# Scores of the third to sixth block: one head's 64 rows at a time, into two banks, instead of a zero-padded operand

## Chip, core and metric

One core of one Trainium2 chip. Times are microseconds on the device for one execution of the program; several executions are timed and their median is given. One further execution is profiled, and all rows below are of that one.

## What is computed

Three stages in a row. The first is a gated linear recurrence over a sequence (a state-space layer) with 4 batches, 8 heads, 768 positions, head width 32 and state width 16; the reference does it in chunks of 32 positions:

```
L = exp(cum[:, None] - cum[None, :]) * causal
M = einsum('bhin,bhjn->bhij', Cc, Bc) * L          # scores times decay
y[:, :, sl] = M @ xc + (Cc @ state) * exp(cum)     # within the chunk + from the state
state = decay_full * state + sum_j B_j x_j * decay_from_j
```

The heads are joined to 3072 tokens of 256 features. Then comes an RMS norm and a gated MLP (256 to 1536 and back, silu), then a second MLP (256 to 2048 and back, softplus). All inputs are fp32.

## The kernel before

**Tiling.** The recurrence runs in chunks of 128 positions: 6 blocks of the sequence by 4 batches are 24 *units*, unit u being block u // 4 of batch u % 4. The two MLPs run over 6 blocks of 512 tokens, one per four units. Their matrices are split into a high and a low part of a short-mantissa fp32 type (F32R), and a product is made of matmuls of high by high, low by high and high by low parts, each with 128 rows, 128 columns of weights and 512 streamed columns. They are the bulk of TensorE's work: PSUM tiles `p` (first layers) and `t` (second layers).

**A unit** (`unit`, L536). It loads the decays of 8 heads (`ab`), scans them into triangles of running products (L607), computes the scores of the 8 heads (L631 to L647), multiplies scores and decays (L656, *decay*, two halves `s` of four heads), and then runs a group *products* (L677 to L695): `inter` (state times C, one matmul per half of the heads, on 64 rows each), `state` and `intra` (32 columns of weights each). From the third block on, two units share one group of products. The scores' two PSUM banks (`gps`) and the products' two banks (`ybanks`) come from one pool `a` of two banks.

**Scores before.** Units 0 to 7 are *native* (`nat`): per head a matmul of 16 rows (the state width) in fp32, which the chip does as two passes. Units 8 to 23, the third to sixth block, use F32R pieces that `split` (L521) has written to DRAM (`parts`): per unit 128 rows by 4 pairs of heads by 128 positions for the one operand (`st`), and as much for the other (`cz`). The upper 64 rows are one head of each pair, the lower 64 the other; within a half, a row is a state index and one of four pieces of the split product. So that one matmul of 128 rows can do both heads of a pair without mixing them, `cz` holds each half of the rows beside zeros: it is 128 rows by 4 pairs by 2 by 128, where `cz[64z:64z+64, q, z]` holds data (L584, two loads) and the rest is zeroed once by GpSimd at the start (L1146). The four matmuls (`pairs`, L643) stream 256 columns each, both heads of pair q side by side. Two pairs go to each bank, so a bank holds the heads in another order than `ab` does; the decay reads `ab` by a rearranged view (L654) and counts both halves of `ab` as read and written (L657). Two `cz` tiles take turns; at the end of the program they hold MLP operands (L950).

**Order.** Every operation is registered with its engine, an estimated time, a rank, and what it reads and writes. A planner (`Plan`) simulates the engines, picks an order for each queue from ranks and due times in eight passes, and keeps the best. At the start (`LEAD`, `plan.now`) an order written by hand holds. TensorE (PE), VectorE (DVE), ScalarE (ACT) and GpSimd (POOL) each run their own list in order. Nearly all DMAs are issued by one queue, SP. The planner's estimate for a set of `pairs` is 4 x 125 ns (L647).

Of the kernel before, what the change touches and what calls it, by code (L numbers as in the profile page):

```python
# [8 lines left out]
F32R = mybir.dt.float32r  # L9
# [5 lines left out]
ALU = mybir.AluOpType  # L15
AX = mybir.AxisListType

P = 128
NB, NH, SEQ, HD, NS = 4, 8, 768, 32, 16
# [308 lines left out]
def tile_ssd_then_swiglu_then_softplus_mlp(  # L328
# [10 lines left out]
    nc = tc.nc  # L339
    act, dve, pool, pe = nc.scalar, nc.vector, nc.gpsimd, nc.tensor  # L340
    plan = Plan(LAT)
# [4 lines left out]
    def buf(tag, shape, dt=F32, bufs=1):  # L346
        if bufs not in pools:
            pools[bufs] = ctx.enter_context(tc.tile_pool(name=f"sb{bufs}", bufs=bufs))
        return plan.buf(pools[bufs], bufs, tag, shape, dt)
# [5 lines left out]
    def pbuf(tag, shape):  # L355
        p, n = {"p": (ps_p, 4), "a": (ps_a, 2), "t": (ps_t, 2)}[tag]
        return plan.buf(p, n, tag, shape, F32)

    def mm(o, l, r, start, stop):
        pe.matmul(out=o, lhsT=l, rhs=r, start=start, stop=stop, skip_group_check=True)  # L360
# [12 lines left out]
    def PE(ns, rank, fn, r=(), w=(), cols=0):  # L373
        plan.op({"pe": (ns, fn)}, rank, r, w, cols)
# [7 lines left out]
    def pool_ns(n):  # L382
        return 150 + n * 2.1

    def DVE(n, rank, fn, r=(), w=(), fast=False, port=True, ns=None):
        plan.op({"dve": (ns or dve_ns(n, fast), fn) + (("port",) if port else ())}, rank, r, w)
# [4 lines left out]
    def POOL(n, rank, fn, r=(), w=()):  # L391
        plan.op({"pool": (pool_ns(n), fn, "port")}, rank, r, w)
# [14 lines left out]
    def LOAD(kb, rank, fn, w, r=()):  # L407
        plan.op({"sp": (kb * DMA_NS, fn)}, rank, r, w)
# [13 lines left out]
    cz = [const.tile([P, 4, 2, P], F32, name=f"cz{i}") for i in range(2)]  # L422
# [9 lines left out]
    parts = [dram.tile([2, P, 4, 4 * P], F32, name=f"parts{t}") for t in range(UPB)]  # L432
# [17 lines left out]
    for layer, t in seq:  # L450
        b = blocks[t]
# [84 lines left out]
    def unit(u):  # L536
        nat = u < NATIVE
        blk, b = divmod(u, NB)
# [6 lines left out]
        def at(name):  # L545
            plan.now = None if blk_of[u] else LEAD[name][o]
        rank = [base]

        def nxt(k=1):
            rank[0] += k * step  # L550
# [4 lines left out]
        R = rank[0] - 12 if blk_of[u] else -100 + b  # L555
        plan.now = None if blk_of[u] else LOADS + 2 + o

        if blk_of[u] == 0 and o >= 2:
            abt = buf(("xxh", "xxl")[b - 2], [P, 2, 4 * P], F32, 3)
            xbt = buf("s", [P, 4 * P], F32, N_S)  # L560
        else:
            abt = buf("ab", [P, 2, 4 * P], F32, N_AB)
            xbt = buf("xc", [P, DM + 3 * P], F32, N_XC)
        spread_a = u < SPREAD
        if not spread_a:
            LOAD(512, R, lambda: nc.sync.dma_start(out=abt().rearrange("p s f -> p (s f)"), in_=a_clip[u].to_broadcast([P, 8 * P])),
                 [abt, (abt, 0), (abt, 1)], ["a_clip"] + ["normed"] * (blk == 2))
        zc, zk = cz[u % 2], ("cz", u % 2)
        if nat:

            if b % 2 == 0:
                pair_of[blk, b + 1] = pair_of[blk, b] = buf("hw", [P, 2, 4 * P], F32, N_H)
            bct, r0 = pair_of[blk, b], 32 * (b % 2)
            for s in range(2):
                rows16 = bc[blk].rearrange("(k n) w f -> k n w f", n=NS)[2 * b + s]
                LOAD(64, R, lambda s=s, rows16=rows16: nc.sync.dma_start(out=bct()[r0 + 64 * s:r0 + 64 * s + NS], in_=rows16), [(bct, b % 2, s)],
                     () if first else ["a_clip"])
        else:
            st = buf("st", [P, 4 * P], F32, 2)
            LOAD(256, R, lambda: nc.sync.dma_start(out=st(), in_=parts[blk][0].rearrange("(b k) s f -> b (k s) f", b=NB)[b]),  # L580
                 [st], [("parts", blk, 0), ("parts", blk, 1)])
            for z in range(2):
                half = parts[blk][1].rearrange("(b z k) s (q i) -> b z (k s) q i", b=NB, z=2, q=4)[b, z]
                LOAD(128, R, lambda z=z, half=half: nc.sync.dma_start(out=zc[64 * z:64 * z + 64, :, z], in_=half), [(zk, z)],  # L584
                     [("parts", blk, 2), ("parts", blk, 3), ("zero", u % 2)])
        nx = DM + (1 if first else 2) * P
        LOAD(nx / 2, R, lambda: nc.sync.dma_start(out=xbt()[:, 0:nx], in_=xc[u, :, 0:nx]), [xbt, (xbt, "c")],
             () if first else ["a_clip"])
# [25 lines left out]
        if not first:  # L614
# [3 lines left out]
                out=sm()[:, 0:P].rearrange("p (g c) -> p g c", g=2), in0=S[b]().rearrange("p (o c) -> p o c", o=1).to_broadcast(  # L618
                    [P, 2, 2 * HD]), in1=mask.rearrange("p (g c) -> p g c", g=2), op=ALU.mult), [S[b], "cst"], [sm])
# [11 lines left out]
        gps = [pbuf("a", [P, 4 * P]) for _ in range(2)]  # L631
        at("scores")
        if nat:

            def scores():
                for q in range(4):
                    c = slice(q * P, (q + 1) * P)
                    for z in range(2):
                        rows = slice(r0 + 64 * z, r0 + 64 * z + NS)
                        mm(gps[z]()[:, c], bct()[rows, 0, c], bct()[rows, 1, c], True, True)  # L640
            PE(820, rank[0], scores, [(bct, b % 2, 0), (bct, b % 2, 1)], list(gps), 512)
        else:
            def pairs():  # L643
                for q in range(4):
                    mm(gps[q // 2]()[:, q % 2 * 2 * P:(q % 2 + 1) * 2 * P], st()[:, q * P:(q + 1) * P].bitcast(F32R),
                       zc[:, q].rearrange("p z i -> p (z i)").bitcast(F32R), True, True)
            PE(4 * 125, rank[0], pairs, [st, (zk, 0), (zk, 1)], list(gps), 1024)  # L647
        for s in range(2):
            gp = gps[s]

            def decay(gp=gp, s=s):
                m, g = abt()[:, s], gp()
                if not nat:
                    m = abt()[:, :, 2 * s * P:(2 * s + 2) * P].rearrange("p z (q i) -> p q z i", q=2)  # L654
                    g = g.rearrange("p (q z i) -> p q z i", q=2, z=2)
                dve.tensor_tensor(out=m, in0=m, in1=g, op=ALU.mult)  # L656
            ak = [(abt, 0), (abt, 1)] if not nat else [(abt, s)]  # L657
            at(f"decay{s}")
            DVE(512, rank[0], decay, ak + [gp], ak, port=False)
            nxt(2)  # L660
# [35 lines left out]
        if not last:  # L696
# [4 lines left out]
            else:  # L701
                DVE(64, rank[0], lambda: dve.scalar_tensor_tensor(out=S[b](), in0=S[b](), scalar=pr()[:, P - 1:P],
                    in1=sp(), op0=ALU.mult, op1=ALU.add), [S[b], ys, (xbt, "p")], [S[b]])
# [8 lines left out]
        c = slice(o * P, (o + 1) * P)  # L712
# [4 lines left out]
        elif j == nj - 1:  # L717
            c = slice((o - j) * P, (o + 1) * P)
# [223 lines left out]
    def halves(b, view):  # L942
        return [lambda k=k: view(b)[:, k * 4 * P:(k + 1) * 4 * P].bitcast(F32R) for k in range(2)]

    def place(d, i):

        wo = lambda k: ([lambda s=s: W["wo"][s][:, 2 * k:2 * k + 2].rearrange("p a k f -> p (a k f)") for s in (0, 1)],
                        [("wo", k, 0), ("wo", k, 1)], [])
        if i < 2 and d:
            return halves(cz[i], lambda b: b.rearrange("p a z i -> p (a z i)")), [("cz", i, "h"), ("cz", i, "l")], [(("cz", i), z) for z in range(2)]  # L950
        if d:
            return wo(i - 2)
        if i < 2 or i == 6:
            b = buf("wr", [P, 8 * P + 64], I32, N_W)
            return halves(b, lambda b: b()), [(b, "h"), (b, "l")], []
        b = buf("xx" + "hl"[i % 2], [P, KD, 4 * P], F32R, 3)
        b.rank = duo_at[0] - 20 + i // 2
        return halves(b, lambda b: b().rearrange("p k i -> p (k i)")), [(b, "h"), (b, "l")], []
# [130 lines left out]
    with tc.manual_schedule():  # L1089
# [5 lines left out]
            out=ident4[:, P:4 * P].rearrange("p (o i) -> p o i", o=3),  # L1095
            in_=ident.rearrange("p (o i) -> p o i", o=1).to_broadcast([P, 3, P]), func=ACTF.Copy), ["eye"], ["ident"])
# [44 lines left out]
        plan.now = 2.7  # L1141
        for i in range(2):
            POOL(180, -103, lambda i=i: pool.memset(zz[i], 0.0), (), [("zz", i)])
        plan.now = 6.1
        for i in range(2):
            POOL(370, -1 + i, lambda i=i: pool.memset(cz[i], 0.0), (), [("zero", i)])  # L1146

        wp.append(pbuf('p', [P, 4 * P]))
        for i in range(FILL):
# [53 lines left out]
def _launch(arrays):  # L1203
    import numpy as np
    import concourse.bacc as bacc
    from concourse.bass_utils import run_bass_kernel_spmd

    nc = bacc.Bacc("TRN2", target_bir_lowering=False, num_devices=1, dynamic_dma_scratch_size=1024)
    args, feed = [], {}
    for name, a in arrays.items():  # L1210
        a = np.ascontiguousarray(a)
        feed[f"in_{name}"] = a
        args.append(nc.dram_tensor(f"in_{name}", a.shape, mybir.dt.from_np(a.dtype), kind="ExternalInput").ap())
    args.append(nc.dram_tensor("out_y", (KD, P, NT), F32, kind="ExternalOutput").ap())
    with tile.TileContext(nc) as tc:
        tile_ssd_then_swiglu_then_softplus_mlp(tc, *args)
    return run_bass_kernel_spmd(nc, [feed], core_ids=[0]).results[0]["out_y"]
# [47 lines left out]
```

## Time and profile before

| what | value |
|---|---|
| median of 3 runs | 592.0 us (591.65 to 592.43) |
| the profiled execution | 592.1 us |
| its span, first to last instruction | 590.3 us |
| PE busy | 584.9 us, 99% |
| DVE busy | 414.3 us, 70% |
| ACT busy | 334.4 us, 57% |
| POOL busy | 20.1 us, 3% |
| mean granted TensorE clock | 0.999 of full speed |

PE is TensorE's stream of matmuls, PEld its loads of weights. A busy share is taken over the whole span, which has stages with different limits. The ends of matmuls are modelled and they overlap (an MLP matmul is shown with 379 ns, and the next one starts after 216), so for TensorE the distances from start to start tell more than durations. A row of the timeline merges instructions of one kind that follow each other; its duration goes from the first start to the last end.

### The profile page before, as it was taken

The numbers are of one execution on the slowest core, as the hardware profiler recorded it, in microseconds if no ns is written. First come the engines' busy times: TensorE is split into PE (matmuls) and PEld (weight loads), VectorE is DVE, ScalarE is ACT, GpSimd is POOL, SyncE is SP. The second block draws the span as 40 slices with busy tenths as digits, with TensorE's granted clock in tenths as the row PEclk, the third lists the DMA queues.
The fourth block names the chain that finished last, engine by engine and source line by source line (L and its number), as shares of the span: only waits on it lengthen the run. The fifth ranks groups of instructions, "written<-read, shape, count | busy, mean of one in ns | idle before, by whom it ended". The sixth has DMA issues, their size and how long they took to land.

```text
span 590.3 us, 8851 instructions
## 1 busy us (share of the span) xinstructions
PE 584.9 (99%) x3337; PEld 504.6 (85%) x3337; DVE 414.3 (70%) x683; ACT 334.4 (57%) x603; POOL 20.1 (3%) x41
## 2 busy tenths in 40 slices
PE   9999999999999999999999999999999999999997
PEld 7888888888888888888888888888888888888885
DVE  6899989588879478687977773464399754555453
ACT  2667655578686546435534433443377765767574
POOL 3300000000000000000000000000000000000000
PEclk9999999999999999999999999999999999999999
DMA  7576757567788734343330000000000000100001
GB/s 207 181 223 195 228 185 251 141 214 241 264 240 288 225 113 143 93 139 110 93 117 2 0 1 1 0 1 0 1 1 1 1 1 0 72 1 1 1 1 71
DMA packets 33434, 59.75 MB, mean 101 GB/s; under 512 B 3120, under 2 KB 14960, under 8 KB 33392
## 3 DMA queue, kind: packets, MB, share of 16 engines
q1 hardware_dynamic: 33248, 58.93, 30.8%
q8 instruction: 26, 0.43, 0.3%
q10 hardware_dynamic: 144, 0.26, 0.1%
q14 instruction: 16, 0.13, 0.1%
HBM read 47.45 MB, written 11.73 MB: 100 GB/s over the span
## 4 chain that ended last, share of the span: by engine, by line
PE 97%; DVE 2%; ACT 0%; issue 0%
PE p L360 53%; PE t L360 30%; PE a L360 13%; DVE hw L403 0%; DVE st L1023 0%; DVE s L1050 0%; DVE ab L989 0%; DVE wol L970 0%; DVE st L1019 0%; DVE s L397 0%; DVE st L397 0%; ACT hw L396 0%; DVE zz L397 0%; DVE wgl L403 0%; ACT s L396 0%
## 5 line engine op out<-in xcount | busy, mean ns | idle before, releaser
L396 ACT ACTIVATE hw<-s 128x512 fp32r<-128x512 f32 x168 | 105.7, 629 | 90.4 <-DVE s L872 67.9
L403 DVE TENSOR_TENSOR hw<-s,hw 128x512 fp32r<-128x512 f32 x168 | 115.4, 687 | 53.5 <-ACT hw L396 52.3
L360 PE MATMUL t<-hw,woh 128*128 128x512 f32 x288 | 86.4, 382 | 0.0
L872 DVE TENSOR_TENSOR s<-s,p 128x512 f32<-128x512 f32 x72 | 49.2, 685 | 50.2 <-PE p L360 45.8
L360 PE MATMUL t<-hw,wph 128*128 128x512 f32 x256 | 76.5, 380 | 0.0
L868 ACT ACTIVATE s<-p 128x512 f32<-128x512 f32 x72 | 42.9, 595 | 55.6 <-PE p L360 55.4
L360 PE MATMUL p<-xxh,wgh 128*128 128x512 f32 x168 | 64.0, 382 | 0.0
L360 PEld LDWEIGHTS t<-hw,woh 128*128 128x128 f32 x288 | 53.6, 189 | 8.6 <-issue 1.2
L360 PE MATMUL p<-xxh,wgl 128*128 128x512 f32 x156 | 59.2, 380 | 0.0
L360 PE MATMUL p<-xxh,wvh 128*128 128x512 f32 x152 | 57.7, 380 | 0.0
L360 PE MATMUL p<-xxh,wvl 128*128 128x512 f32 x148 | 56.1, 379 | 0.0
L360 PE MATMUL t<-hw,wol 128*128 128x512 f32 x144 | 54.6, 379 | 0.0
L360 PEld LDWEIGHTS t<-hw,wph 128*128 128x128 f32 x256 | 47.7, 189 | 7.0 <-issue 0.6
L607 DVE TENSOR_TENSOR_SCAN ab<-ab,ident 128x512 f32<-128x512 f32 x40 | 48.6, 1223 | 2.1 <-DMA ab<-a_clip 2.1
L360 PE MATMUL t<-hw,wpl 128*128 128x512 f32 x128 | 48.5, 379 | 0.0
L360 PE MATMUL p<-xxl,wgh 128*128 128x512 f32 x156 | 47.4, 379 | 0.0
L1055 ACT ACTIVATE s<-s 128x512 f32<-128x512 f32 x48 | 30.0, 625 | 25.8 <-DVE s L1050 25.6
L360 PE MATMUL p<-xxl,wvh 128*128 128x512 f32 x148 | 44.3, 379 | 0.0
L360 PE MATMUL a<-hw,wph 128*128 128x512 f32 x128 | 39.1, 382 | 0.4 <-ACT hw L396 0.3
L360 PEld LDWEIGHTS p<-xxh,wgh 128*128 128x128 f32 x168 | 31.7, 189 | 4.8 <-issue 0.4
L1050 DVE TENSOR_TENSOR s<-xc,p 128x512 f32<-128x512 f32 x32 | 22.0, 686 | 16.9 <-PE p L360 11.9
L360 PEld LDWEIGHTS p<-xxl,wgh 128*128 128x128 f32 x156 | 29.5, 189 | 4.3 <-ACT xc L396 0.2
(209 smaller groups left out, 1030.1 us busy)
## 6 DMA issues: line engine op xcount, KB each, us to landing
wr<-in_w SPq DMA_DIRECT2D x34, 512.0 KB
ab<-a_clip SPq DMA_DIRECT2D x20, 512.0 KB
parts<-wr SPq DMA_DIRECT2D x16, 512.0 KB
xc<-in_xc SPq DMA_DIRECT2D x20, 256.0 KB
st<-parts SPq DMA_DIRECT2D x16, 256.0 KB
cz<-parts SPq DMA_DIRECT2D x32, 128.0 KB
out_y<-s SPq DMA_DIRECT2D x11, 256.0 KB
wr<-in_bc SPq DMA_DIRECT2D x8, 256.0 KB
```

Of the source, the lines that this page charges most:

```text
L360: pe.matmul(out=o, lhsT=l, rhs=r, start=start, stop=stop, skip_group_check=True)
L396: ways = {"act": (act_ns(n), lambda: act.activation(out=out(), in_=in_(), func=ACTF.Copy)), "dve": (dve_ns(n, sbuf), lambda: dve.tensor_co ...
L403: return lambda: eng.tensor_tensor(out=out(), in0=in_(), in1=f32(hi()), op=ALU.subtract)
L607: DVE(512, rank[0], lambda t=t, d=d: dve.tensor_tensor_scan(out=t(), data0=d(), data1=ident4, initial=0.0, op0=ALU.mult, op1=ALU.add), dk ...
L868: ACT(n, rank - EPI, lambda: act.activation(out=s()[:, 0:n], in_=ps[0]()[:, 0:n], func=ACTF.Silu), [ps[0]], [s, "table"] if new_table else ...
L872: DVE(n, rank - EPI, lambda: dve.tensor_tensor(out=s()[:, 0:n], in0=s()[:, 0:n], in1=ps[1]()[:, 0:n], op=ALU.mult), [s, ps[1]], [s], port= ...
L1050: DVE(n, r - EPI, lambda: dve.tensor_tensor(out=s(), in0=x(), in1=y(), op=ALU.add), xk, [s], port=False)
L1055: ACT(n, r - EPI, lambda: act.activation(out=s(), in_=in_(), func=ACTF.Softplus), rk, [s, "table"] if new else [s], 1283 if new else 0)
```

## The change

For units 8 to 23 the zero padding goes. The second operand is loaded as it lies in `parts`, with one DMA of 256 KB instead of two of 128 KB, into the first half of the same `cz` tile. Each of the four matmuls becomes two: one head's 64 rows of `st` and of `cz`, 128 streamed columns, head half z into bank z. These are eight matmuls, on the upper and the lower 64 rows in turn. Each bank then has its heads in the order of `ab`, so the decay uses plain views and touches one half of `ab` only. The two memsets go. The planner's estimate of a set becomes 350 ns and 512 columns.

```diff
@@ -565,7 +565,7 @@
         if not spread_a:
             LOAD(512, R, lambda: nc.sync.dma_start(out=abt().rearrange("p s f -> p (s f)"), in_=a_clip[u].to_broadcast([P, 8 * P])),
                  [abt, (abt, 0), (abt, 1)], ["a_clip"] + ["normed"] * (blk == 2))
-        zc, zk = cz[u % 2], ("cz", u % 2)
+        zc, zk = lambda: cz[u % 2][:, 0:2].rearrange("p a z i -> p (a z i)"), ("cz", u % 2)
         if nat:
 
             if b % 2 == 0:
@@ -579,10 +579,8 @@
             st = buf("st", [P, 4 * P], F32, 2)
             LOAD(256, R, lambda: nc.sync.dma_start(out=st(), in_=parts[blk][0].rearrange("(b k) s f -> b (k s) f", b=NB)[b]),
                  [st], [("parts", blk, 0), ("parts", blk, 1)])
-            for z in range(2):
-                half = parts[blk][1].rearrange("(b z k) s (q i) -> b z (k s) q i", b=NB, z=2, q=4)[b, z]
-                LOAD(128, R, lambda z=z, half=half: nc.sync.dma_start(out=zc[64 * z:64 * z + 64, :, z], in_=half), [(zk, z)],
-                     [("parts", blk, 2), ("parts", blk, 3), ("zero", u % 2)])
+            LOAD(256, R, lambda: nc.sync.dma_start(out=zc(), in_=parts[blk][1].rearrange("(b k) s f -> b (k s) f", b=NB)[b]), [zk],
+                 [("parts", blk, 2), ("parts", blk, 3)])
         nx = DM + (1 if first else 2) * P
         LOAD(nx / 2, R, lambda: nc.sync.dma_start(out=xbt()[:, 0:nx], in_=xc[u, :, 0:nx]), [xbt, (xbt, "c")],
              () if first else ["a_clip"])
@@ -642,19 +640,18 @@
         else:
             def pairs():
                 for q in range(4):
-                    mm(gps[q // 2]()[:, q % 2 * 2 * P:(q % 2 + 1) * 2 * P], st()[:, q * P:(q + 1) * P].bitcast(F32R),
-                       zc[:, q].rearrange("p z i -> p (z i)").bitcast(F32R), True, True)
-            PE(4 * 125, rank[0], pairs, [st, (zk, 0), (zk, 1)], list(gps), 1024)
+                    c = slice(q * P, (q + 1) * P)
+                    for z in range(2):
+                        rows = slice(64 * z, 64 * z + 64)
+                        mm(gps[z]()[:, c], st()[rows, c].bitcast(F32R), zc()[rows, c].bitcast(F32R), True, True)
+            PE(350, rank[0], pairs, [st, zk], list(gps), 512)
         for s in range(2):
             gp = gps[s]
 
             def decay(gp=gp, s=s):
-                m, g = abt()[:, s], gp()
-                if not nat:
-                    m = abt()[:, :, 2 * s * P:(2 * s + 2) * P].rearrange("p z (q i) -> p q z i", q=2)
-                    g = g.rearrange("p (q z i) -> p q z i", q=2, z=2)
-                dve.tensor_tensor(out=m, in0=m, in1=g, op=ALU.mult)
-            ak = [(abt, 0), (abt, 1)] if not nat else [(abt, s)]
+                m = abt()[:, s]
+                dve.tensor_tensor(out=m, in0=m, in1=gp(), op=ALU.mult)
+            ak = [(abt, s)]
             at(f"decay{s}")
             DVE(512, rank[0], decay, ak + [gp], ak, port=False)
             nxt(2)
@@ -947,7 +944,7 @@
         wo = lambda k: ([lambda s=s: W["wo"][s][:, 2 * k:2 * k + 2].rearrange("p a k f -> p (a k f)") for s in (0, 1)],
                         [("wo", k, 0), ("wo", k, 1)], [])
         if i < 2 and d:
-            return halves(cz[i], lambda b: b.rearrange("p a z i -> p (a z i)")), [("cz", i, "h"), ("cz", i, "l")], [(("cz", i), z) for z in range(2)]
+            return halves(cz[i], lambda b: b.rearrange("p a z i -> p (a z i)")), [("cz", i, "h"), ("cz", i, "l")], [("cz", i)]
         if d:
             return wo(i - 2)
         if i < 2 or i == 6:
@@ -1141,9 +1138,6 @@
         plan.now = 2.7
         for i in range(2):
             POOL(180, -103, lambda i=i: pool.memset(zz[i], 0.0), (), [("zz", i)])
-        plan.now = 6.1
-        for i in range(2):
-            POOL(370, -1 + i, lambda i=i: pool.memset(cz[i], 0.0), (), [("zero", i)])
 
         wp.append(pbuf('p', [P, 4 * P]))
         for i in range(FILL):
```

## Rows read from the trace of the kernel before

**Rows 1.** Stretch, us: busy us (instructions) of PE, PEld, DVE, ACT, POOL; clock, DMA.
```profile
120.00:315.00 195.00, 195.00 (x1275) 168.81 (x1274) 157.26 (x258) 111.64 (x203) 7.03 (x14) 1.00 0.53 173
```

**Rows 2.** The page's span, and the chain that ended last.
```profile
span 590.3 us, 8851 instructions
...
PE 97%; DVE 2%; ACT 0%; issue 0%
```

**Rows 3.** Tile `a`: kinds, xcount, ns min/median/max, first and last start in us.
```profile
L360 PEld LDWEIGHTS a<-xc,Sm x80: 182/186/188, 39.2 to 312.6; 64*128 64x128 f32 x80
...
L360 PEld LDWEIGHTS a<-cz,st x64: 187/189/192, 121.0 to 308.7; 128*128 128x128 f32 x64
L360 PE MATMUL a<-cz,st x64: 274/282/288, 121.2 to 308.9; 128*128 128x256 f32 x64
```

**Rows 4.** TensorE's timeline (start us, us, kind): the first, third and last set.
```profile
120.98 0.38 PE L360 MATMUL t<-hw,wol 128*128 128x512 f32 x1
121.20 0.64 PE L360 MATMUL a<-cz,st 128*128 128x256 f32 x4
121.67 0.38 PE L360 MATMUL p<-xxh,wgh 128*128 128x512 f32 x1
121.89 0.38 PE L360 MATMUL p<-xxh,wgl 128*128 128x512 f32 x1
...
150.13 0.64 PE L360 MATMUL a<-cz,st 128*128 128x256 f32 x4
...
308.51 0.64 PE L360 MATMUL a<-cz,st 128*128 128x256 f32 x4
308.98 0.59 PE L360 MATMUL t<-hw,woh 128*128 128x512 f32 x2
```

**Rows 5.** TensorE's timeline, products of two units.
```profile
133.38 0.59 PE L360 MATMUL p<-xxl,wvh 128*128 128x512 f32 x2
133.90 0.72 PE L360 MATMUL a<-xc,Sm 64*128 64x128 f32 x8
134.55 0.43 PE L360 MATMUL a<-xc 128*32 128x64 f32 x16
```

**Rows 6.** TensorE's timeline, native scores of unit 7.
```profile
66.10 0.38 PE L360 MATMUL t<-hw,wol 128*128 128x512 f32 x1
66.41 1.16 PE L360 MATMUL a<-hw 16*128 16x128 f32 x16
67.50 0.48 PE L360 MATMUL p<-xxh,wgh 128*128 128x512 f32 x1
67.82 0.38 PE L360 MATMUL p<-xxh,wgl 128*128 128x512 f32 x1
```

**Rows 7.** TensorE's timeline, products of one unit.
```profile
39.20 0.49 PE L360 MATMUL a<-xc,Sm 64*128 64x128 f32 x4
39.62 0.32 PE L360 MATMUL a<-xc 128*32 128x64 f32 x8
```

**Rows 8.** POOL's timeline at the start.
```profile
12.41 1.84 POOL L1146 MEMSET cz<- 128x1024 f32 x2
14.33 0.40 POOL L1133 TENSOR_SCALAR s<-s 96x256 f32<-96x256 f32 x1
15.17 0.56 POOL L803 TENSOR_TENSOR rs<-rs,small 128x1 f32<-128x1 f32 x1 [0.44 <-DMA a_clip<-Sm]
```

**Rows 9.** ACT's timeline at the start.
```profile
14.91 0.17 ACT L801 ACTIVATE rs<-p 128x1 f32<-128x1 f32 x1 [0.71 <-PE p L360]
```

**Rows 10.** The DMA queue SP's timeline behind the first set.
```profile
122.24 1.18 SPq L584 DMA_DIRECT2D cz<-parts  x2
```

**Rows 11.** DVE's decay groups, to 100 us, then 115 to 315.
```profile
L656 DVE TENSOR_TENSOR ab<-ab,a 128x512 f32<-128x512 f32 x12 | 7.9, 680 | 0.2
...
L656 DVE TENSOR_TENSOR ab<-ab,a 128x512 f32<-128x512 f32 x32 | 21.5, 682 | 0.5
```

**Rows 12.** DVE's timeline behind the last set.
```profile
309.97 0.69 DVE L656 TENSOR_TENSOR ab<-ab,a 128x512 f32<-128x512 f32 x1
```

## The prediction

> **What bounds the kernel now.** I read the stretches first, to find which engine has no idle time where the change lies, then the chain of waits, then single score sets on TensorE's timeline. From 120 to 315 us, where all sixteen changed score sets stand, PE is busy 195.00 of 195.00 us, while DVE has 157.26 and ACT 111.64 [rows 1]. The reader is to see that PE's column equals the length of the stretch: there is no hole into which a longer set could go, and none that a shorter one would leave. The chain that ended last says the same, 97% PE [rows 2]. So whatever the change adds to or takes from TensorE's own stream in this stretch moves the end one for one, and DVE, ACT, POOL and the DMA queue matter only if they come to hold TensorE up. The granted clock there is 1.00, the 2.4 GHz level [rows 1].
>
> A busy PE is not a PE at its peak, so durations are of no use here: I count from start to start of neighbouring matmuls.
>
> **The old set.** The 64 matmuls of `pairs` are 16 sets of four [rows 3], the first at 121.20 and the last at 308.51 [rows 4]. All sixteen stand alone between MLP matmuls of 128 rows, 128 columns of weights and 512 columns streamed. The first: last MLP matmul before it at 120.98, first of the set at 121.20, next MLP matmul at 121.67, the one after it at 121.89 [rows 4]. From 120.98 to 121.89 are 0.91 us. Two MLP matmuls alone, without a set, take the same two steps in 2 x 0.216 = 0.432 (the steps from 121.67 on are 0.21 to 0.22). So the old set costs 0.91 - 0.43 = 0.478 us; the last one, 308.51 to 308.98, has the same 0.47. That is four times 0.119 for 256 streamed columns, and nothing at either edge: entering takes 0.22 and leaving 0.12, the plain streaming of the matmul before.
>
> **The new set.** Eight matmuls, each with 64 rows and 128 columns of weights and 128 streamed columns, on rows 0 to 63 and 64 to 127 in turn. No such set with this operand type stands in the trace. The nearest rows are the inter-chunk products (`a<-xc,Sm`): 64 rows, the two halves in turn, 128 columns of weights, 128 streamed columns, into two banks. They are ordinary fp32, so each matmul of the program is two passes; the x8 of [rows 5] are eight instructions, which is the count the new set has in one pass each. Three prices follow.
>
> First, the edges. The MLP matmul before that x8 starts at 133.59 (the second of the two merged from 133.38: 133.38 + 0.59 - 0.38) and the x8 at 133.90: 0.31 where 0.216 is usual. The native scores (16 rows) show it too: 66.10 to 66.41 going in, and on the way out 67.50 to 67.82 between the first and second MLP matmul, 0.32 instead of 0.216 [rows 6]. So going in costs 0.09 and the restart 0.10, and between them the last tiled matmul holds the next 128-row one off for about 0.20 us (below).
>
> Second, the body. Four instructions of the kind (two pairs of halves) take 39.20 to 39.62 = 0.42 to the next group [rows 7], eight take 133.90 to 134.55 = 0.645 [rows 5], sixteen of the native scores 66.41 to 67.50 = 1.09 [rows 6]. Each further pair costs 0.225/2 = 0.112, and what is left for x8, 0.645 - 3 x 0.112 = 0.31, is the first weight load, which nothing covers, and the way out. The halves do run together (a pair costs 0.112, not 0.22), but 0.112 per pair is no less than the 0.119 of one old matmul: a weight load of 128 columns is shown as 186 ns for 64 rows and 189 for 128 [rows 3], so halving the rows doesn't shorten it, and there are four pairs of loads as there were four loads.
>
> Third, the sum. 0.31 (in) + 0.645 (body and way out) + 0.32 (restart) = 1.275, less the same 0.432, is 0.843 us. Against 0.478 the set is 0.365 us longer; sixteen sets, 5.8 us. One thing may make it shorter: the rows are passes of ordinary fp32, the new matmuls are single passes of the type that streamed 256 columns in 0.119 us, so 128 columns would take some 0.06 rather than 0.11. Within the body that is hidden behind the weight loads, behind the last pair it is not: up to 0.05 less per set, 0.315 and 5.0 us in all. I take 0.345, near the row: 16 x 0.345 = **5.5 us**.
>
> The Trainium skill, page "TensorEngine Tiling (Array Packing)", section "Key Properties", says that changing the tiling mode, not merely the tile, drains the engine. By that rule every one of the sixteen sets pays two drains that the old sets did not, which is the sign the rows give; the page has no price for it, and the 0.09, 0.20 and 0.10 are this trace's.
>
> **The rest of the change**, at nothing:
> - POOL's two memsets go, 12.41 to 14.25. Behind them on POOL stand the clip at 14.33 and the power at 15.17 [rows 8]; but the power takes the mean that ACT ends at 14.91 + 0.17 = 15.08 [rows 9], so it stays where it is, and the chain of [rows 2] lists no POOL. Bounds: from 0 to -1.8 us, the memsets' whole length; I take 0.
> - 32 loads of 128 KB become 16 of 256 KB on SP's queue, about 0.6 us of issue less per unit. The load of a unit follows the matmuls that free its tile at once, 122.24 behind the set at 121.20, and that tile is read at 150.13: 28 us of cover [rows 4, 10]. The queue saves some 10 us of issues that nothing waits for: 0, and with the cover gone it would be a microsecond per unit at most.
> - The decay's operands turn from a strided to a plain order. The plain form of the native units takes 680 ns, the strided one 682 [rows 11]: 0. Its first half now waits for the whole set, not for half of it, some 0.5 us later; the last unit's first decay starts at 309.97, 1.46 us behind its set [rows 4, 12]: covered, and the products behind the decays move with TensorE's stream, so their slack stays.
> - The planner gets the set at 350 ns instead of 500 and fewer loads, so it writes some orders anew. In a stretch where PE never idles an exchange of MLP matmuls costs nothing; a set next to the 64-row products would share their edges, but both take the whole of the two-bank pool "a" with the decays in between, so that can't happen. I leave 1 us to either side for this.
>
> The profiled execution took 592.1, its span of 590.3 [rows 2] and 1.8 around it; + 5.5 = 597.6. The median of the runs is 592.0, 0.1 below the profiled one, so I say **597.5 us**, with 596 to 599 as this case's own range.
>
> **Rivals.**
> 1. *The edges cost nothing here* (the other side). The first halves' weights are loaded while the last MLP matmul streams, and the first MLP weights while the last pair streams, as they are between all 128-row sets, and single-pass halves of 128 columns stream in 0.06 a pair. Then a set is 4 x 0.06 = 0.24 against 0.478: -3.8 us, 588.2; if the loads keep 0.112 per pair, 0.45 against 0.478: -0.5 us, 591.5, no change. It decides from the point at which the edges together cost less than 0.03 (loads at 0.112) or 0.24 (at 0.06). For it: the new operands are single-pass like the MLP's, and no row shows a single pass in 64-row sets. Against: every tiled group in the trace, 16 rows or 64 rows, has the same 0.31 and 0.32 at its edges, and the MLP matmuls on the other side of them are single-pass already. The Trainium skill, "TensorE: Matmul & The Clock Gate", section "Measured speedup vs the span model", prices a pack of tiles as one matmul and 4 ns per further tile; that would be this rival's first form, and the 7 instructions of [rows 5] behind the first agree with it only inside the body. Chances: 0.06 faster, 0.06 no change.
> 2. *The halves run one behind the other*, or a single pass of only 128 columns streams slowly. Each pair then takes up to 0.22: 4 x 0.11 = 0.44 more per set, 7.1 in all, 604.6. For it: no single-pass matmul with fewer than 256 columns is in the trace. Against: pairs of halves at 0.112 in [rows 5 to 7]. Chance 0.07.
> 3. *TensorE comes to wait* for a decay, a load or a PSUM bank in a new order of the planner, 1 to 3 us on top: 599 to 601. Against: 195.00 of 195.00 busy with DVE at 81% [rows 1]. Chance 0.06.
>
> **How the numbers follow.** The forecast has 0.75. A measurement of this kernel can tell about 0.2% (1.2 us) from no change. Slower: 0.75 + 0.07 + 0.06 = 0.88; within: 0.06; faster: 0.06. For eight in ten I need the forecast's own range and a part of rival 3 above and of a smaller price at the edges below: 595 to 600.
>
> **What would show it.** In the profile after: 128 matmuls of 64 rows and 128 columns in place of 64 of 256; from the MLP matmul before a set to the second one after it 1.22 to 1.28 us instead of 0.91; 0.31 on the way in and 0.32 between the first two MLP matmuls behind; 0.11 from pair to pair; PE still without idle time from 120 to 320; DVE, ACT and POOL as before but for the two memsets. It is wrong if that distance is at or under 0.91, or over 1.5, or if the 64-row sets stand next to the products; and its argument is wrong if the end moves by other than sixteen times the difference.

## The result, and the profile after

The changed kernel took 596.73 us in the median (596.42 to 597.66, 4 runs) against 592.02 (591.65 to 592.43): a ratio of 1.0082, 95% interval 1.0064 to 1.0099, so 3.8 to 5.9 us slower. The forecast was 597.5, range 595 to 600. The profiled execution has a span of 595.2 us, 4.9 more than before [rows 2].

The stretch with all score sets first (columns as in [rows 1]), then the page's span and the chain that ended last:

```profile
120.00:320.00 200.00, 200.00 (x1307) 168.62 (x1306) 155.27 (x250) 110.85 (x198) 7.70 (x14) 1.00 0.51 168
```

```profile
span 595.2 us, 8955 instructions
...
PE 97%; DVE 2%; ACT 0%; issue 0%
```

TensorE is still without a hole where the sets stand, at the same granted clock (1.00, the 2.4 GHz level), and the chain is still 97% PE: what the sets grow by, the end moves by.

The rows of tile `a` that answer to [rows 3], and TensorE's timeline around the first and the last set, which answers to [rows 4]:

```profile
L360 PEld LDWEIGHTS a<-cz,st x128: 182/187/188, 121.2 to 318.0; 64*128 64x128 f32 x128
L360 PE MATMUL a<-cz,st x128: 268/272/326, 121.2 to 318.1; 64*128 64x128 f32 x128
```

```profile
120.85 0.38 PE L360 MATMUL t<-hw,wol 128*128 128x512 f32 x1
121.16 0.66 PE L360 MATMUL a<-cz,st 64*128 64x128 f32 x8
121.75 0.48 PE L360 MATMUL p<-xxh,wgh 128*128 128x512 f32 x1
122.07 0.38 PE L360 MATMUL p<-xxh,wgl 128*128 128x512 f32 x1
...
317.40 0.38 PE L360 MATMUL t<-hw,wol 128*128 128x512 f32 x1
317.71 0.66 PE L360 MATMUL a<-cz,st 64*128 64x128 f32 x8
318.31 0.70 PE L360 MATMUL t<-hw,woh 128*128 128x512 f32 x2
```

From the MLP matmul before the set to the second one behind it are 122.07 - 120.85 = 1.22 us, 0.91 before. It splits into 0.31 going in, 0.59 from the set's first matmul to the MLP, and 0.32 between the first two MLP matmuls. All sixteen sets lie between 1.220 and 1.224. Less the 0.432 of the two MLP steps, the sixteen sum to 12.63 us; the old ones summed to 7.61. The difference, **5.0 us**, is the result. The remaining terms of the span: the first MLP matmul starts 0.41 us earlier (29.41 against 29.82), and one native set at 56.93 is 0.28 longer, because its second matmul starts 0.21 behind the first instead of 0.01. 5.02 - 0.41 + 0.28 = 4.89 of the 4.9. Neither of these two shows as the change's doing: the start varies from execution to execution (experiment 4), and in experiments 3 and 4, which have the changed kernel's order on TensorE, that native set takes 1.09 again.

```profile
56.93 1.44 PE L360 MATMUL a<-hw 16*128 16x128 f32 x16
58.30 0.48 PE L360 MATMUL p<-xxh,wvh 128*128 128x512 f32 x1
```

(66.41 to 67.50 are 1.09 for such a set in [rows 6]; here it is 1.37.)

### The profile page after: what moved, and what is told of

Read it like the earlier page. It is cut to its first block, busy times and chain, and to the rows that moved or that the text cites. A ratio compares the mean times of both kernels' runs of the same rounds, so it can differ in the third digit from the quotient of the medians.

```text
span 595.2 us, 8955 instructions
## 1 busy us (share of the span) xinstructions
PE 589.8 (99%) x3401; PEld 504.0 (85%) x3401; DVE 415.7 (70%) x684; ACT 334.6 (56%) x602; POOL 18.8 (3%) x39
## 4 chain that ended last, share of the span: by engine, by line
PE 97%; DVE 2%; ACT 0%; issue 0%
PE p L360 53%; PE t L360 30%; PE a L360 14%; DVE hw L403 0%; DVE st L1020 0%; DVE s L1047 0%; DVE ab L986 0%; DVE wol L967 0%; DVE st L1016 0%; DVE s L397 0%; DVE st L397 0%; ACT hw L396 0%; DVE zz L397 0%; DVE wgl L403 0%; ACT s L396 0%
```

## The experiments

Theory A is the prediction's: TensorE pays for going into a 64-row set and out of it, and within it weight loads set the pace. Rival B: the time follows the number of matmuls, eight instead of four. Rival C: it is the order that the planner writes for its new numbers. Each experiment was compared with the kernel before, run in turn with it on the same chip.

**1. The planner's numbers alone.**

```diff
 # kernel before
-            PE(4 * 125, rank[0], pairs, [st, (zk, 0), (zk, 1)], list(gps), 1024)
+            PE(350, rank[0], pairs, [st, (zk, 0), (zk, 1)], list(gps), 512)
```

> The kernel before, with only the planner's numbers for a score set changed as in the change (350 ns and 512 columns instead of 500 and 1024); the matmuls, loads and memsets stay. Theory A (the time goes to the edges of the 64-row sets on TensorE): the old sets keep their 0.48 us each and PE stays without idle time from 120 to 315 us, so 592.0 +- 0.6 us. Theory C (the new order of the planner costs it): up to the whole 4.7 us, 595 to 597. Theory B (eight instructions instead of four): 592.0, as A.

592.76 us against 591.71, ratio 1.0013 (1.0005 to 1.0022). The old sets keep their cost (16 sum to 7.57 us). Rival C is not the 4.7 us, but it is not nothing: the new order costs 0.3 to 1.3 us, a little over what A allowed. In the profiled execution the span is 0.7 longer; 0.48 of it is a later first MLP matmul (30.30), and 0.27 a matmul at 236.36 that comes 0.17 late and the restart behind it. Whether the later start belongs to the order is open (see experiment 4). This order is not the changed kernel's either; what that one costs is read there, under experiment 4.

**2. Eight matmuls without a 64-row tile.**

```diff
 # kernel before
-                    mm(gps[q // 2]()[:, q % 2 * 2 * P:(q % 2 + 1) * 2 * P], st()[:, q * P:(q + 1) * P].bitcast(F32R),
-                       zc[:, q].rearrange("p z i -> p (z i)").bitcast(F32R), True, True)
+                    for z in range(2):
+                        at0 = (q % 2 * 2 + z) * P
+                        mm(gps[q // 2]()[:, at0:at0 + P], st()[:, q * P:(q + 1) * P].bitcast(F32R), zc[:, q, z].bitcast(F32R), True, True)
```

> The kernel before, with each 128-row matmul of 256 columns split into two of 128 columns on the same 128 rows of weights: eight matmuls and eight weight loads of 128 columns per set, no 64-row tile anywhere in it, so no edges. Theory A holds that a weight load of 128 columns paces the body at 0.11 us whatever its rows: 8 x 0.11 = 0.88 per set instead of 0.48, +0.40, sixteen sets +6.4 us: 598.4, with 0.216 going in and no 0.32 behind. If matmuls are paced by their 128 streamed columns (some 0.06): 8 x 0.06 = 0.48, 592.0. Theory B (the time follows the number of matmuls): eight cost here what they cost in the changed kernel, +0.31 per set, 597.

598.62 us, ratio 1.0117 (1.0103 to 1.0131). TensorE's timeline around its last set:

```profile
313.88 0.59 PE L360 MATMUL p<-xxl,wgh 128*128 128x512 f32 x2
314.31 1.00 PE L360 MATMUL a<-cz,st 128*128 128x128 f32 x8
315.15 0.65 PE L360 MATMUL t<-hw,woh 128*128 128x512 f32 x2
```

The reader is to see two things. Going in costs the usual 0.216 (the second of the two merged starts at 314.09, the set at 314.31): no edge there. And eight matmuls take 0.84 to the next MLP matmul, the first step 0.06 and the others 0.11: 128 streamed columns alone would allow 0.06, and the later ones are held to the pace of the weight loads (more on this under "The body"). That is A's pace of 0.11 in a set of 128 rows. B's 597 lies outside the interval (597.8 to 599.5 on its 591.7), and the forms differ: the same eight matmuls are dearer here in the middle, free at the entry, and cost 0.05 behind (0.27 between the two MLP matmuls that are merged from 315.15).

**3. All eight on one half of the rows.**

```diff
 # changed kernel
-                        rows = slice(64 * z, 64 * z + 64)
-                        mm(gps[z]()[:, c], st()[rows, c].bitcast(F32R), zc()[rows, c].bitcast(F32R), True, True)
+                        rows = slice(0, 64)
+                        mm(gps[z]()[:, c], st()[rows, c].bitcast(F32R), zc()[rows, c].bitcast(F32R), True, True)
```

> The changed kernel, with all eight matmuls of a set on rows 0 to 63 of both operands: the second half's heads get the first half's scores, so part of the output is not the reference's. Same instructions, same order, same edges; only the halves can no longer run together. Theory A: seven steps of 0.11 instead of three after the first, 4 x 0.11 = 0.44 more per set, +7.0 us on the changed kernel's 596.7: 603.7. If the halves gain nothing from being on different rows: 596.7.

604.03 us, ratio 1.0211 (1.0195 to 1.0227), 7.3 over the changed kernel.

```profile
314.24 1.10 PE L360 MATMUL a<-cz,st 64*128 64x128 f32 x8
315.28 0.48 PE L360 MATMUL p<-xxh,wgh 128*128 128x512 f32 x1
315.60 0.38 PE L360 MATMUL p<-xxh,wgl 128*128 128x512 f32 x1
```

1.04 from the set's first matmul to the MLP instead of 0.59: 0.45, four steps of 0.11. The order of every engine is the changed kernel's. So in the changed kernel the two halves do load and stream together, and that is worth 7 us; the edges are not what this run changes, and 0.32 behind stays.

**4. The memsets put back.**

```diff
 # changed kernel
+        plan.now = 6.1
+        for i in range(2):
+            POOL(370, -1 + i, lambda i=i: pool.memset(cz[i], 0.0), (), [("cz", i)])
```

> The changed kernel, with the two GpSimd memsets of cz put back at their place (the first loads of cz then wait for them). Theory A with its step on POOL: no operation that the chain needs stands behind them, so 596.7 +- 0.5 us, the profile's first score set no earlier or later than by the spread of the start of runs. If the memsets had held up the start: up to 1.8 us later, 598.5.

596.93 us, ratio 1.0089 (1.0075 to 1.0102); the changed kernel has 1.0082. Its first MLP matmul starts at 29.32, without memsets at 29.41. Over the ten profiles of this study it starts between 29.22 and 30.30, with the memsets (29.82, 30.30, 29.36, 29.32, 29.98) and without (29.41, 29.22, 29.69, 30.03, 29.38) alike. The 0.41 us of the ledger above lies within this spread, so it is not put down to the change. This run also shows what the changed kernel's order costs, since TensorE's order is the same: from the first MLP matmul to the end of the span it takes 594.8 - 29.32 = 565.5 us, the kernel before 590.3 - 29.82 = 560.5. The 5.0 between them is the sets' 5.0, which leaves nothing for rival C.

**5 and 6. The same extra matmul, outside the set or inside it.**

```diff
 # changed kernel, in front (5)
+                mm(gps[1]()[:, 2 * P:4 * P], mean.to_broadcast([P, P]).bitcast(F32R), mean.to_broadcast([P, 2 * P]).bitcast(F32R), True, True)
                 for q in range(4):
 # changed kernel, in the middle (6)
                 for q in range(4):
+                    if q == 2:
+                        mm(gps[1]()[:, 2 * P:4 * P], mean.to_broadcast([P, P]).bitcast(F32R), mean.to_broadcast([P, 2 * P]).bitcast(F32R), True, True)
```

> The changed kernel, with one more 128-row matmul of 256 columns (a constant) ahead of each score set, written to a place that the set then overwrites. It stands on the MLP side of the edge, so the number of edges stays. Theory A: going in to it 0.216, from it into the set 0.205 as behind a 256-column matmul elsewhere in the trace, so +0.11 per set, +1.8 us on 596.7: 598.5. Theory B (count of matmuls): the same.

> The same extra matmul between the second and third pair of each set: the same number of matmuls and columns as with it in front, but each set now has twice the edges. Theory A: 0.31 + 0.17 + 0.20 + 0.31 + 0.17 + 0.20 + 0.32 = 1.68 from the MLP matmul before to the second one after, instead of 1.33 with it in front: +0.345 x 16 = 5.5 us more than extra_front, 604.0. Theory B: as extra_front, 598.5.

In front: 598.67 us, ratio 1.0115 (1.0100 to 1.0131). In the middle: 604.49, ratio 1.0213 (1.0199 to 1.0227). One set of the first, then one of the second:

```profile
291.68 0.38 PE L360 MATMUL t<-hw,wol 128*128 128x512 f32 x1
291.90 0.27 PE L360 MATMUL a<-mean 128*128 128x256 f32 x1
292.10 0.66 PE L360 MATMUL a<-cz,st 64*128 64x128 f32 x8
292.69 0.48 PE L360 MATMUL p<-xxh,wgh 128*128 128x512 f32 x1
293.01 0.38 PE L360 MATMUL p<-xxh,wgl 128*128 128x512 f32 x1
```

```profile
296.60 0.38 PE L360 MATMUL t<-hw,wol 128*128 128x512 f32 x1
296.91 0.44 PE L360 MATMUL a<-cz,st 64*128 64x128 f32 x4
297.27 0.38 PE L360 MATMUL a<-mean 128*128 128x256 f32 x1
297.58 0.44 PE L360 MATMUL a<-cz,st 64*128 64x128 f32 x4
297.95 0.48 PE L360 MATMUL p<-xxh,wgh 128*128 128x512 f32 x1
298.27 0.38 PE L360 MATMUL p<-xxh,wgl 128*128 128x512 f32 x1
```

1.33 and 1.67 us for the same nine matmuls. The sixteen sets differ by 5.45 us, the medians by 5.8 and the spans of the two profiled executions by 5.9, of which 0.34 is a later start (30.03 against 29.69). Rival B gives the two the same time and falls here. One more way in and out costs 0.34 us.

**7. Two sets in one: half the edges.** The score sets of the two units of a pair are one operation of sixteen matmuls; the first unit takes two banks of pool `p`.

```diff
 # changed kernel
-        gps = [pbuf("a", [P, 4 * P]) for _ in range(2)]
+        gps = [pbuf("a" if nat or j else "p", [P, 4 * P]) for _ in range(2)]
...
-            PE(350, rank[0], pairs, [st, zk], list(gps), 512)
+            held.append((pairs, [st, zk], list(gps)))
+            if j == nj - 1:
+                two = list(held)
+
+                def both():
+                    for x in two:
+                        x[0]()
+                PE(350 * len(two), rank[0], both, sum((x[1] for x in two), []), sum((x[2] for x in two), []), 512 * len(two))
+                held.clear()
```

The first unit's decays are registered behind that operation.

> The changed kernel, with the score sets of the two units that share a group of products written as one set of sixteen matmuls; the first unit takes its two banks from pool p. Half the edges, the same matmuls. Theory A: 0.31 + 0.165 + 6 x 0.11 + 0.20 + 0.32 = 1.66 per two units, less 0.43, is 1.23 instead of 2 x 0.79 = 1.58: -0.345 x 8 = -2.8 us on 596.7: 593.9, if the MLP does not wait for the banks lent; still over the kernel before. Theory B: 596.7.

595.80 us, ratio 1.0068 (1.0056 to 1.0081): 0.9 less than the changed kernel, not 2.8. The first merged set, and further on the place where most of the rest went:

```profile
125.50 0.59 PE L360 MATMUL p<-xxl,wvh 128*128 128x512 f32 x2
126.03 0.66 PE L360 MATMUL p<-cz,st 64*128 64x128 f32 x8
126.53 0.61 PE L360 MATMUL a<-cz,st 64*128 64x128 f32 x8
127.07 0.70 PE L360 MATMUL t<-hw,woh 128*128 128x512 f32 x2
...
139.39 0.38 PE L360 MATMUL t<-hw,wol 128*128 128x512 f32 x1
140.54 0.70 PE L360 MATMUL t<-hw,wph 128*128 128x512 f32 x2 [0.77 <-DVE xxl L943]
```

The sets do what A says: no edge between the two halves of sixteen, 1.67 from the MLP matmul before (125.72) to the second one behind (127.39), eight sets with 9.9 us instead of 12.63: -2.7. The span is 1.0 shorter only, because the new order lets TensorE wait: behind 139.39 for 0.93 us on DVE's work on the low part of a finished MLP block (`xxl`), at two more places 0.12 and 0.17, with the restarts behind them 1.6 us in all, and 0.44 inside two groups of products. So A's price per edge holds, and its "if" did not.

**8. Fewer edges elsewhere, in the kernel before.** Only `PAIRS = 2` became `PAIRS = 1`: the units of the second block of tokens share their products too.

> The kernel before (128-row score sets), with two units sharing one group of products from the second block of tokens on instead of the third: two groups of tiled matmuls and their edges fewer, the matmuls themselves as many. A group of one unit takes 738 + 1208 - 309 = 1.64 us from the MLP matmul before to the second one after, less 0.43 is 1.21 (rows of the kernel before); one of two units 961 + 1756 - 202 - 432 = 2.08. If edges add up as in the other runs: 2 x (2 x 1.21 - 2.08) = -0.7 us, 591.3 against 592.0, if the first blocks' MLP does not wait for the later norm. If it waits: no change or slower by the wait, 592 to 594.

593.97 us, ratio 1.0054 (1.0033 to 1.0074): slower. (My sum there was off: a group of one unit takes 738 + 1208 - 209 = 1.74 us, not 1.64, so the edges would have given -1.1.) Its executions fall into two kinds, five at 593.6 to 594.0 and four at 597.3 to 598.3; the profiled one is of the second. A wait on TensorE's timeline, and the stretches:

```profile
67.14 0.48 PE L360 MATMUL t<-hw,woh 128*128 128x512 f32 x1 [0.98 <-DVE hw L403]
```

```profile
60.00:64.00 4.00, 3.39 (x15) 2.35 (x14) 4.00 (x5) 1.39 (x3) 0.00 (x0) 1.00 0.69 193
64.00:67.50 3.50, 2.52 (x23) 1.72 (x22) 3.50 (x7) 1.42 (x2) 0.00 (x0) 1.00 0.90 300
67.50:74.20 6.70, 6.70 (x28) 5.11 (x27) 5.38 (x11) 3.16 (x5) 0.00 (x0) 0.50 0.17 57
```

DVE is busy throughout from 60 to 67.5 us and TensorE waits for it there, 1.6 us of idle time; that is more than the edges give. From start to start the three matmuls that wait come 2.2 us late in all, twice the edges' 1.1. What follows is below. No version that was run beats the kernel before.

## Why the prediction was right, and where a term was off

**What bounds.** Right: PE without idle time in the stretch, and the end moved by the difference of the sets (sets 5.0 us, span 4.9, medians 4.7).

**The edges.** Right, and shown: 0.31 and 0.32 stand at all sixteen sets; experiment 6 doubles the edges for 0.34 us each, experiment 7 halves them and each saved one takes 0.34 off. The rule of the Trainium skill, page "TensorEngine Tiling (Array Packing)", section "Key Properties", that a change of tiling mode drains the engine, agrees with these: 0.34 us for one way in and out, a price that the page doesn't give. Where the 0.34 lies is seen on TensorE's weight loads; the first line is the kernel before, the others are the changed kernel:

```profile
120.98 0.64 PEld L360 LDWEIGHTS a<-cz,st 128*128 128x128 f32 x4
...
121.16 0.52 PEld L360 LDWEIGHTS a<-cz,st 64*128 64x128 f32 x8 [0.33 <-issue]
121.75 0.19 PEld L360 LDWEIGHTS p<-xxh,wgh 128*128 128x128 f32 x1
121.86 0.19 PEld L360 LDWEIGHTS p<-xxh,wgl 128*128 128x128 f32 x1
```

Before, the set's first load starts together with the MLP matmul ahead of it (120.98), 0.22 before the set's first matmul. In the changed kernel it starts with the set itself (121.16, the MLP matmul ahead at 120.85), and the load for the MLP matmul behind the set starts with that matmul (121.75). So on both sides nothing is loaded ahead. The price is 0.09 more on the way in, 0.05 more to the second pair (0.165 instead of 0.11), 0.09 more from the last pair to the MLP matmul (0.20 instead of 0.11) and 0.10 in the restart, where the second load starts only 0.11 behind the first. A slower restart by itself also comes without a 64-row set: it is 0.27 in experiment 2 and 0.30 in the next rows.

**The body.** Right: 0.11 per pair of halves. Experiment 3 shows that the halves run together, experiment 2 that 128 columns of weights, not the 128 streamed columns, set the 0.11. The trace has a row with hardly any streaming that says the same, eight full-height matmuls with 128 columns of weights each and one streamed column (changed kernel):

```profile
76.55 0.95 PE L360 MATMUL a<-mean,xxh 128*128 128x1 f32 x8
77.36 0.46 PE L360 MATMUL p<-xxh,wgh 128*128 128x512 f32 x1
77.65 0.38 PE L360 MATMUL p<-xxh,wgl 128*128 128x512 f32 x1
```

They take 0.81 us to the MLP matmul: 0.03 for the first step and 0.11 for each of the seven others.

**The sum** was 5.5, its lower end 5.0, and the sets gave 5.0. The mis-sized term is the gain of a single pass: I gave it 0.02 of its possible 0.05 per set and put it "behind the last pair". It came in full, and elsewhere. TensorE's timeline of the changed kernel, at the first set's second pair, its last pair, and the second pair of an inter-chunk group that starts at 134.39:

```profile
121.33 0.39 PE L360 MATMUL a<-cz,st 64*128 64x128 f32 x4
...
121.55 0.28 PE L360 MATMUL a<-cz,st 64*128 64x128 f32 x2
...
134.60 0.39 PE L360 MATMUL a<-xc,Sm 64*128 64x128 f32 x4
```

The second pair starts 0.17 behind the first (121.16) where the two-pass rows have 0.21, and from the last pair to the MLP matmul it is 121.75 - 121.55 = 0.20, the same as behind the two-pass groups. So a shorter last matmul does not shorten the way out. Why it is 0.20 either way is not shown by these runs.

**The terms at nothing.** The memsets: right; the power on POOL still follows its mean from ACT, at 14.76 behind 14.50 + 0.17 [rows 8, 9], and experiment 4 has the time unchanged. The loads: SP issues one load of 0.38 us where two took 1.18 [rows 10], and nothing waits for it. The decay: 681 ns, 680 and 682 before [rows 11].

```profile
14.76 0.56 POOL L800 TENSOR_TENSOR rs<-rs,small 128x1 f32<-128x1 f32 x1 [2.22 <-ACT rs L798]
```

```profile
14.50 0.17 ACT L798 ACTIVATE rs<-p 128x1 f32<-128x1 f32 x1 [0.71 <-PE p L360]
```

```profile
122.30 0.38 SPq L582 DMA_DIRECT2D cz<-parts  x1
```

```profile
L653 DVE TENSOR_TENSOR ab<-ab,a 128x512 f32<-128x512 f32 x32 | 21.1, 681 | 1.8 <-PE a L360 1.5
```

**The planner** at 1 us to either side: its order for the changed kernel cost nothing that can be seen (experiment 4); the order of experiment 1 cost 0.3 to 1.3 us.

**The rivals.** Edges at no cost: fell with every set. What the prediction reads from [rows 5] for that rival holds only within a pair: of the seven instructions behind the first, the four second halves start 0.01 us behind their first halves, but from pair to pair it is 0.21, 0.11 and 0.11. Halves in a row: fell, experiment 3 is what it would have looked like. TensorE waiting in a new order: not in the changed kernel, but it is what took most of the gain in experiment 7 and, in the profiled execution, more than the gain in experiment 8.

## What to carry to other kernels

A full-height matmul half filled with zeros can be cheaper than two half-height ones without them: here a pair costs 0.111 us tiled, paced by its weights' 128 columns, and 0.119 padded, while the one way into the tiled form and out of it costs 0.34. (What sets the 0.119 these runs don't part: 256 streamed columns are half of the MLP's 0.216, and a weight load allows 0.11.) A tiled set of four pairs gains 0.03 us inside and pays ten times that at its edges; so count the edges of a short tiled set before its columns, from start to start. And where TensorE has no idle time, removing edges by merging sets only pays if the order that comes of it makes nothing wait.

## What was not expected of the hardware

In experiment 8 the granted clock fell from 1.00 to 0.50 (1.2 GHz) from 67.50 to 74.20 us and then rose again. Before it fell, TensorE had been busy 5.91 of 7.50 us, in pieces between waits for DVE; in the kernel before the same 7.5 us are fully busy and the clock stays. Matmuls of 512 columns then follow each other at 0.43 us instead of 0.216, so about 3.3 us are lost in the 6.7. That is near the distance between the two kinds of executions, some 3.8. The clock goes with the kind in all nine: its mean over the execution is 0.994 in each of the four longer ones, as 6.7 us at half the clock in a span of 596.5 would make it, and 0.999 or 1.000 in the five shorter. None of the shorter kind was profiled, so it is not shown that the clock is the whole of the distance, nor why only four of nine executions of one kernel lose it.
